# Windowed attention with a gated convolution layer on one core: where the probabilities are normalised and transposed, and in which form the value product writes x

## The chip, the cores and the metric

The kernel runs on one core of a Trainium2 chip. PE is TensorE (matmuls and transposes, results in the eight banks of PSUM), DVE is VectorE, ACT is ScalarE, SP only issues loads. The metric is device time in microseconds (us): the median of several executions. A profile is one more execution, taken by the hardware profiler; its span goes from the first to the last instruction.

## The reference, cut to what matters

Eight batches of eight heads with 64 channels; 512 local and 32 global positions. A local query attends to the 32 global keys and to local keys at most 32 positions away; a global query attends to everything. The 576 rows of each batch then go through a gated layer with 512 channels.

```python
s_l = np.concatenate([s_lg, np.where(np.abs(i - j) <= 32, s_ll, -1e9)], axis=-1)
e = np.exp(s_l - s_l.max(-1, keepdims=True))
a_l = e / (e.sum(-1, keepdims=True) + 1e-9)
out_l = a_l @ np.concatenate([v_g, v_l], axis=2)     # out_g likewise, over all 544 keys
x = rows of (out_g, out_l), heads side by side       # 576 x 512 for each batch
gate = sigmoid(sum(conv_w[k] * xp[:, k:k + S, :] for k in range(5)))   # causal, xp padded in front
out = (gate * (x @ w_val)) @ w_out
```

## The kernel before, in words

**Units.** The work on local queries is cut into 32 units u: one batch and two heads (128 channels). The 512 queries of a unit are 16 chunks of 32; each chunk sees 128 keys, 32 global ones and 96 local ones. A half h of a unit is one head.

**Steps of a unit**, by the names of the order: `s` (l_s, L581): the scores, 32 fp32 matmuls on tiles of 64 rows and 32 columns. `mx` (l_max, L593): DVE adds the mask, negates and writes the rows to `pm` in SBUF, with the row minimum. `exp` (l_exp, L600): ACT, in place. `t` (l_t, L606): PE transposes `pm` into PSUM, four 128x128 for each half. `tc` (l_tc): a copy to `pts` in SBUF, on ACT (L416) or DVE (L418). `av` (l_av, L617): 32 matmuls with the probabilities as weights (128 x 32) and 65 columns of v; the 65th is a column of ones, so the row sums come out beside the products. `den`, `rec` (L626, L630): their reciprocals. `norm` (l_norm, DVE L640 or eight small ACT operations L638): products times reciprocals, to `xs` in SBUF. `xt` (l_xt, L646): four PE transposes. `xc` (l_xc): a copy of the transposed x to SBUF. `halo`: the four columns ahead of it.

**The gated layer.** `xh`, `xl` (L678) split x into two fp32r parts. `tap` and four `conv` steps (L682, scalar_tensor_tensor over 128x512) make the convolution on DVE; for units 0 and 1 (NPC = 2) PE makes it by five matmuls with diagonal matrices (`pc`, L707; diagonals by ACT, L696). `sig` is the sigmoid. For each group of four units (a batch), `g1` (L731) multiplies x by w_val in 16 parts of three matmuls (xh·wvh, xl·wvh, xh·wvl); `gv`, `gh`, `gl` (L739, L745) multiply by the gate and split; `g2` (L771) multiplies by w_out in the same way; `ob` copies the result out of PSUM, and `st` stores it. The 32 global queries of each batch have their own steps (`gs`, `gmax`, `gexp`, `gt`, `gtc`, `gav`, `gden`, `grec`, `gnorm`, `gx`, `gxc`), and their rows go through the gated layer at the very end (g1.g, g2.g).

**What sets the order.** A string ORDER (L61 to L159) lists all steps, with PSUM banks behind @ and, where there is a choice, the engine behind a colon. A class Plan goes through it with costs, and from them puts zero-fills of PE into early gaps; the order of each engine is that of the string. Loads go over SP in the order of the string; pools give buffers in rings (`pm` three, `pts` two, `xs` one).

```python
on_pe(T.matmul(ax[32 * j:32 * j + 32, h, E1 * i:E1 * i + E1], pts[:, h, i, 32 * j:32 * j + 32],
         vt[:, block_win(4 * i + j), h, :], start=True, stop=True))
```

Of the kernel before, what the change touches and what calls it, by code (L numbers as in the profile page):

```python
# [76 lines left out]
t7.0@4 w7.s0:ACT w7.s1 g2.0.0.0@0 gtc1.1 tc7.0 gh.0.2 norm6 w6.s6 t7.1@2 w7.s2 w6.s7 tc7.1 gav1.1 xh4 gl.0.2 w7.s3 iq10
w6.high iv9 gden1 xc5 av7@6 den7 xt6@4 xh5 iq11 w7.s4 rec7 g2.0.0.1 grec1 w7.s5 gnorm1 gh.0.3 w7.s6 norm7:ACT gl.0.3
g2.0.0.2 s8@12 s9@53 gx1@6 xt7@7 w7.s7 w7.high mx9.0 tap4:ACT g2.0.0.3 gxc1 g2.0.1.0@5 mx9.1 g2.0.1.1 exp9.1 g2.0.1.2
t9.1@3 halo4 mx8.0 iv8 mx8.1 g2.0.1.3 xl4 ob.0.0 exp8.1 tc9.1 tap5:ACT conv4.0 halo5:ACT g2.0.2.0@6 ob.0.1:DVE conv4.1  # L80
gs2@20 gmax2.0 t8.1@5 conv4.2 st.0.0 exp8.0 st.0.1 g2.0.2.1 exp9.0 iv11 g2.0.2.2 t8.0@2 g2.0.2.3 g2.0.3.0@3 tc8.0 tc8.1
t9.0@5 gexp2.0 g2.0.3.1 xl5 ob.0.2 conv5.0 gmax2.1 tc9.0 av8@0 conv5.1 conv4.3 conv5.2 xc6 tap6 iv10 halo6:ACT conv5.3
av9@4 gexp2.1 s10@62 den8 rec8 den9 norm8 xh6:DVE gt2.0@0 xc7 xt8@7 gtc2.0 g2.0.3.2 xh7 iq12 mx10.0 mx10.1 halo7 xl6
exp10.0 g2.0.3.3 exp10.1 iq13 conv6.0 s11@26 tap7:ACT rec9 norm9 mx11.0 exp11.0 gav2.0@0 gt2.1@4 g1.1.0.0@1 mx11.1
t10.1@2 conv6.1 gtc2.1 t10.0@6 xl7 iq14 g1.1.0.1 g1.1.0.2 tc10.0 iq15 tc10.1 gav2.1 conv6.2 exp11.1 conv7.0 av10@4 iv12
t11.0@2 conv6.3 xc8:DVE conv7.1 gden2 xt9@7 tc11.0 conv7.2 conv7.3 g1.1.0.3 den10 g1.1.1.0@2 sig4 sig5 g1.1.1.1 g1.1.1.2
grec2 gnorm2 g1.1.1.3 ob.0.3:DVE gv.1.0 xc9 gh.1.0 g1.1.2.0@3 rec10 xh8:DVE tap8:ACT iv13 g1.1.2.1 sig6 g1.1.2.2
tap9:ACT t11.1@7 sig7 gx2@6 g1.1.2.3 norm10 xl8 gl.1.0 gv.1.1 gs3@40 gv.1.2 s12@32 gh.1.1:DVE st.0.3 gxc2 gmax3.0 tc11.1
av11@4 iv14 xt10@7 iq16 mx12.0 g1.1.3.0@3 mx12.1 halo8 exp12.0 den11 gl.1.1 exp12.1 g1.1.3.1 g1.1.3.2 gmax3.1 conv8.0
st.0.2 t12.0@2 gexp3.0 conv8.1 rec11 t12.1@6 g1.1.3.3 tc12.1 conv8.2 gv.1.3 s13@01 gh.1.2:DVE tc12.0 mx13.0 gl.1.2  # L90
conv8.3 mx13.1 norm11:ACT av12@2 gt3.0@4 exp13.0 g2.1.0.0@6 iv15 xt11@0 gh.1.3 halo9:ACT gl.1.3 xh9 xl9 den12 g2.1.0.1
xc10 g2.1.0.2 conv9.0 gtc3.0 rec12 g2.1.0.3 g2.1.1.0@7 s14@14 t13.0@5 norm12 tap10 exp13.1 conv9.1 g2.1.1.1 gexp3.1 xh10
mx14.0 conv9.2 g2.1.1.2 exp14.0 tc13.0 conv9.3 xl10 iq17 t13.1@1 g2.1.1.3 xt12@5 g2.1.2.0@2 ob.1.1:DVE mx14.1 halo10
# [984 lines left out]
```

## Time and profile before

| | us |
|---|---|
| three executions, median | 360.92 |
| lowest, highest | 359.85, 362.54 |
| span of the profiled execution | 358.4 |

The page's times are those of the profiled execution, whose span is 2.5 us below the median of the executions; a change is worked out against the span and then set beside the median. Busy time of an engine is the time in which any of its instructions runs; the start-to-start distance of neighbours is shorter than an instruction's length, since its end lies under the next one.

### The profile page before, as it was taken

To read this page: it belongs to the slowest core of one execution; us is meant where nothing else is said; L and a number is where in the kernel's file an instruction comes from. 1 tells how busy PE (TensorE), PEld (TensorE's weight loads), DVE (VectorE), ACT (ScalarE), POOL (GpSimd) and SP (SyncE) were. 2 spreads that over 40 slices of the span, in tenths; PEclk is the share of its full clock that TensorE was granted. 3 is DMA by queue.
4 is the path that set the end of the run, shared out by engine and by line. 5 is a ranking of instruction groups with operands and counts; after the bars stand their busy time and mean duration, and the time that the engine had idled before them with its cause. 6 is when DMAs were issued, how large, how long until landed. Compare 5 with 4: busy or idle time off the path is not lost.

```text
span 358.4 us, 14856 instructions
## 1 busy us (share of the span) xinstructions
PE 351.0 (98%) x6355; PEld 280.3 (78%) x6355; DVE 315.0 (88%) x1079; ACT 252.3 (70%) x630; POOL 0.8 (0%) x7
## 2 busy tenths in 40 slices
PE   8989999999999999999999999999999999999995
PEld 4647678778878788887878887888878888888895
DVE  4899999889989997998999989997897997995972
ACT  2999998996997888956766767976585585542030
POOL 0000000000000000000000000000000000000000
PEclk9999999999999999999999999999999999999999
DMA  8985677778897458822377157930790110020122
GB/s 277 400 327 171 230 267 262 251 231 299 268 302 251 141 183 289 335 92 85 131 266 260 59 202 251 347 131 28 241 381 8 62 58 2 31 89 32 59 77 71
DMA packets 21906, 66.75 MB, mean 186 GB/s; under 512 B 2384, under 2 KB 4944, under 8 KB 21840
## 3 DMA queue, kind: packets, MB, share of 16 engines
q1 hardware_dynamic: 16800, 56.86, 45.8%
q10 hardware_dynamic: 5040, 8.94, 6.8%
q8 instruction: 50, 0.82, 0.9%
q14 instruction: 16, 0.13, 0.1%
HBM read 56.87 MB, written 8.91 MB: 184 GB/s over the span
## 4 chain that ended last, share of the span: by engine, by line
PE 93%; DMA 4%; DVE 2%; ACT 1%; issue 0%; DVEq 0%
PE psum L731 27%; PE psum L771 25%; PE psum L581 8%; PE psum L617 8%; PE psum L606 8%; PE psum L646 4%; PE psum L545 3%; DMA v<-in_vw_dram 3%; PE psum L507 2%; PE psum L707 2%; PE psum L525 2%; PE psum L527 1%; DMA craw<-in_convT_dram 1%; PE psum L756 1%; DVE pm L593 1%; ACT pm L600 0%
## 5 line engine op out<-in xcount | busy, mean ns | idle before, releaser
L600 ACT ACTIVATE pm<-pm,mx 128x128 f32<-128x128 f32 x256 | 80.7, 399 | 16.2 <-DVE mx L593 16.0
L682 DVE SCALAR_TENSOR_TENSOR gate<-xc,cw,gate 128x512 f32<-128x512 f32 x120 | 88.2, 746 | 1.7 <-ACT gate L409 0.9
L593 DVE CUSTOM_DVE_ANT_0 pm<-psum,mask 128x128 f32<-128x128 f32 x256 | 57.6, 285 | 4.5 <-PE psum L581 4.3
L771 PE MATMUL psum<-woh,gh 128*128 128x512 f32 x128 | 53.7, 419 | 0.0
L731 PE MATMUL psum<-xh,wvh 128*128 128x512 f32 x128 | 52.9, 414 | 0.0
L731 PE MATMUL psum<-xl,wvh 128*128 128x512 f32 x128 | 50.7, 396 | 0.0
L731 PE MATMUL psum<-xh,wvl 128*128 128x512 f32 x128 | 50.5, 394 | 0.0
L771 PE MATMUL psum<-woh,gl 128*128 128x512 f32 x128 | 50.2, 392 | 0.0
L771 PE MATMUL psum<-wol,gh 128*128 128x512 f32 x128 | 50.1, 391 | 0.0
L416 ACT COPY pts<-psum 128x512 f32<-128x512 f32 x51 | 29.2, 590 | 15.3 <-PE psum L606 15.1
L606 PE MATMUL psum<-ident,pm 128*128 128x128 f32 x256 | 38.7, 277 | 0.7 <-ACT pm L600 0.7
L606 PEld LDWEIGHTS psum<-ident,pm 128*128 128x128 f32 x256 | 29.8, 140 | 10.7 <-ACT pm L600 2.9
L581 PE MATMUL psum<-qk 64*32 64x128 f32 x2048 | 36.9, 277 | 0.8 <-DMA qk<-in_qk_dram 0.5
L581 PEld LDWEIGHTS psum<-qk 64*32 64x32 f32 x2048 | 28.9, 107 | 9.1 <-issue 4.3
L617 PEld LDWEIGHTS psum<-v,pts 128*32 128x32 f32 x2048 | 30.5, 109 | 6.9 <-issue 3.3
L617 PE MATMUL psum<-v,pts 128*32 128x65 f32 x2048 | 34.5, 221 | 1.2 <-issue 0.8
L739 DVE TENSOR_TENSOR gv<-psum,gate 128x512 f32<-128x512 f32 x32 | 22.0, 687 | 9.3 <-PE psum L731 8.9
L731 PEld LDWEIGHTS psum<-xh,wvl 128*128 128x128 f32 x128 | 24.0, 188 | 5.4
L771 PEld LDWEIGHTS psum<-woh,gl 128*128 128x128 f32 x128 | 24.0, 188 | 5.3
L731 PEld LDWEIGHTS psum<-xh,wvh 128*128 128x128 f32 x128 | 24.1, 189 | 4.6
L731 PEld LDWEIGHTS psum<-xl,wvh 128*128 128x128 f32 x128 | 24.2, 189 | 4.2
L771 PEld LDWEIGHTS psum<-woh,gh 128*128 128x128 f32 x128 | 24.2, 189 | 4.1 <-DVE mx L593 0.2
(118 smaller groups left out, 559.0 us busy)
## 6 DMA issues: line engine op xcount, KB each, us to landing
qk<-in_qk_dram SPq DMA_DIRECT2D x31, 624.0 KB, 4.7
v<-in_vw_dram SPq DMA_DIRECT2D x30, 520.0 KB, 5.7
v<-in_vw_dram SPq DMA_DIRECT2D x30, 455.0 KB, 6.4
out_dram<-ob ACTq DMA_DIRECT2D x32, 256.0 KB, 2.2
wraw<-in_w_val_dram SPq DMA_DIRECT2D x4, 512.0 KB, 12.3
wraw<-in_w_out_dram SPq DMA_DIRECT2D x4, 512.0 KB, 4.6
v<-in_vw_dram SPq DMA_DIRECT2D x2, 975.0 KB, 12.2
qk<-in_qk_dram SPq DMA_DIRECT2D x1, 320.0 KB, 3.2
```

Of the source, the lines that this page charges most:

```text
L416: A.copy(out, in_)
L545: on_pe(T.matmul(ag[SG * c:SG * c + SG, :], pgt[:k, s, SG * c:SG * c + SG], vt[:k, w, h, :], start=(n == 0), stop=(n == len(steps) - 1)))
L581: on_pe(T.matmul((sx, sy)[h][32 * j:32 * j + 32, i, :], qkt[rows, q_col(m):q_col(m) + 32], qkt[rows, k0:k0 + P], start=True, stop=True))
L593: V.tensor_tensor_reduce(out=pm[:, h, i, :], in0=s[:, i, :], in1=mask[:, i, :], op0=ALU.add, op1=ALU.min, scale=-SCALE, scalar=3.0e38, acc ...
L600: A.activation(out=pm[:, h, i, :], in_=pm[:, h, i, :], func=AF.Exp, bias=mx[:, c:c + 1], scale=-1.0)
L606: on_pe(T.transpose(pt[:, i, :], pm[:, h, i, :], ident))
L617: on_pe(T.matmul(ax[32 * j:32 * j + 32, h, E1 * i:E1 * i + E1], pts[:, h, i, 32 * j:32 * j + 32], vt[:, block_win(4 * i + j), h, :], start ...
L646: on_pe(T.transpose(xt[:, P * i:P * i + P], xs[:, i].rearrange("p h d -> p (h d)"), ident))
L682: V.scalar_tensor_tensor(out=acc, in0=xc[:, k:k + SL], scalar=cw[:, u % NDT, k:k + 1], in1=acc, op0=ALU.mult, op1=ALU.add)
L731: on_pe(T.matmul(box["pv", e], w[:, e, t * P:t * P + P], x, start=(t == 0 and q == 0), stop=(t == NDT - 1 and q == 2)))
L739: V.tensor_tensor(out=box["gv", e], in0=box["pv", e], in1=gates[x0 + e], op=ALU.mult)
L771: on_pe(T.matmul(box["po", r], g[:, e, rs], w[:, e, :], start=(e == 0 and q == 0), stop=(e == NDT - 1 and q == 2)))
```

## The change

What it does:
- Row sums come from the exponential itself (`accum_out`), no longer from a column of ones. `den` and `rec` work on them.
- `norm` multiplies the probabilities `pm` in place (a half is 128x512; DVE one operation, or ACT four), ahead of the transpose; 26 halves on DVE and 38 on ACT.
- `t` is now l_turn: DVE transposes the 32x32 blocks of a half (128x512) from `pm` to `pts`. PE's transposes of the probabilities and the `tc` copies are gone.
- `av` takes v as weights (32 keys by 64 channels) and the probabilities as columns, in 52 matmuls with 128, 96, 64 or 32 columns, and writes x transposed, 128 columns in each of four banks. `xt` and `xs` are gone; `xc` reads those four banks, always on ACT.
- The host lays out queries, keys and values anew: qk 768 KB for a unit in one load (before 624; the first unit's in three pieces of 320, 160 and 144), v 455 KB in one load (before 975, in two). Global scores run over 640 columns in place of 544.
- The convolution of units 0 to 3 is on PE (NPC 2 to 4), with ten more diagonals on ACT.
- The ORDER string is a new one, and the Plan is gone: it is run as it stands. DVE has 2 output copies (before 14), 12 gh casts (17), 8 xh casts (9), 7 taps (10), 9 halo copies (14); ACT has the others. 14 loads of ACT's function tables are left of 18, and 12 zero-fills of PE for 15 (beside two short ones, as before).

```diff
-NPC = 2
+NPC = 4
 def load_qk(u):
-        for a, b in zip((EARLY[0], 0, EARLY[1]), (EARLY[1], EARLY[0], QK)) if u == 0 else ((0, QK),):
-            transfer(t[:, a:b], qk[u, :, a:b])
+        transfer(t, qk[u])
...
 def l_exp(u, h):
-            A.activation(out=pm[:, h, i, :], in_=pm[:, h, i, :], func=AF.Exp, bias=mx[:, c:c + 1], scale=-1.0)
+            A.activation(out=pm[:, h, i, :], in_=pm[:, h, i, :], func=AF.Exp, bias=mx[:, c:c + 1], scale=-1.0,
+                         accum_out=mx[:, 8 + c:9 + c])
-    def l_t(u, h):
...
-            on_pe(T.transpose(pt[:, i, :], pm[:, h, i, :], ident))
-    def l_tc(u, h):
-        copy(f"tc{u}.{h}", st[u]["pts"][:, h], st[u]["pt", h])
+    def l_norm(u, h):
+        p, rec = st[u]["pm"][:, h], st[u]["mx"][:, 8 + R * h:8 + R * h + R]
+        if BY[f"norm{u}.{h}"] == "ACT":
+            for i in range(R):
+                A.activation(out=p[:, i, :], in_=p[:, i, :], func=AF.Copy, scale=rec[:, i:i + 1])
+        else:
+            V.tensor_tensor(out=p, in0=p, in1=rec.unsqueeze(2).to_broadcast([P, R, P]), op=ALU.mult)
+    def l_turn(u, h):
...
+        V.transpose(out=st[u]["pts"][:, h].rearrange("p i a q -> p (i a q)"),
+                    in_=st[u]["pm"][:, h].rearrange("p i c -> p (i c)"))
     def l_av(u):
-            for i in range(4):
-                for j in range(4):
-                    on_pe(T.matmul(ax[32 * j:32 * j + 32, h, E1 * i:E1 * i + E1], pts[:, h, i, 32 * j:32 * j + 32],
-                             vt[:, block_win(4 * i + j), h, :], start=True, stop=True))
+        x = st[u]["x"] = banks(f"av{u}", R)[:, :, :P]
+        def product(j, h, slot, first, count, at, step, last):
+            rows = slice(C * j, C * j + C)
...
+            on_pe(T.matmul(x[D * h:D * h + D, j, C * first:C * (first + count)], vt[rows, slot, h, :D], p,
+                           start=(slot == NS - 1), stop=last))
+        for slot in (NS - 1, 2, 3, 1, 4, 0, 5):
+            for n in range(8):
+                j, h = n % R, (n + n // R) % 2
...
-    def l_xt(u):
...
-            on_pe(T.transpose(xt[:, P * i:P * i + P], xs[:, i].rearrange("p h d -> p (h d)"), ident))
     def l_xc(u):
-        copy(f"xc{u}", xc[:, KW - 1:], bank(f"xt{u}"))
+        copy(f"xc{u}", xc[:, KW - 1:].rearrange("p (j q) -> p j q", j=R), st[u]["x"])
```

What stands on DVE before, in the middle of the program, about units 15 to 19 (L682 are convolution steps, L640 the normalisation, L418 a copy or cast, L678 the low part of x, L626 den):

```order
L411 TENSOR_SCALAR gate16_3309<-xc16_3272,cw_68 128x512
L682 SCALAR_TENSOR_TENSOR gate15_3297<-xc15_3063,cw_68,gate15_3297 128x512
L418 CAST xh16_3324<-xc16_3272 128x512
L682 SCALAR_TENSOR_TENSOR gate15_3297<-xc15_3063,cw_68,gate15_3297 128x512
L640 TENSOR_TENSOR xs17_3329<-psum_64,mx17_2846 128x512
L678 TENSOR_TENSOR xl16_3325<-xc16_3272,xh16_3324 128x512
L418 COPY pts19_3262<-psum_64 128x512
L682 SCALAR_TENSOR_TENSOR gate15_3297<-xc15_3063,cw_68,gate15_3297 128x512
L682 SCALAR_TENSOR_TENSOR gate16_3309<-xc16_3272,cw_68,gate16_3309 128x512 x2
L626 TENSOR_SCALAR mx18_3107<-psum_64 128x8
```

And what stands on DVE at the like place of the change (L510 convolution steps, L441 rec, L449 the normalisation of a half, L454 the block transpose):

```order
L510 SCALAR_TENSOR_TENSOR gate15_3210<-xc15_3167,cw_68,gate15_3210 128x512
L510 SCALAR_TENSOR_TENSOR gate14_3260<-xc14_3087,cw_68,gate14_3260 128x512
L441 RECIPROCAL mx16_2684<-mx16_2684 128x8
L510 SCALAR_TENSOR_TENSOR gate14_3260<-xc14_3087,cw_68,gate14_3260 128x512
L449 TENSOR_TENSOR pm17_2938<-pm17_2938,mx17_2939 128x512
L510 SCALAR_TENSOR_TENSOR gate14_3260<-xc14_3087,cw_68,gate14_3260 128x512
L510 SCALAR_TENSOR_TENSOR gate15_3210<-xc15_3167,cw_68,gate15_3210 128x512
L449 TENSOR_TENSOR pm16_2683<-pm16_2683,mx16_2684 128x512
L454 STREAM_TRANSPOSE pts16_3328<-pm16_2683 128x512 x2
```

The copy of transposed probabilities out of PSUM has left DVE, the normalisation reads and writes SBUF, and two block transposes follow it for each unit.

What stands on PE before, about unit 21's scores (L581), with the transposes of x (L646) and of probabilities (L606) among the first products of a batch (L731):

```order
L581 MATMUL psum_64<-qk21_3039 32x128 x32
L646 MATMUL psum_64<-ident_66,xs19_3551 128x128 x4
L731 MATMUL psum_64<-xh15_3070,wvh_74 128x512
L731 MATMUL psum_64<-xl15_3071,wvh_74 128x512
L731 MATMUL psum_64<-xh15_3070,wvl_75 128x512
L606 MATMUL psum_64<-ident_66,pm20_3494 128x128 x4
L731 MATMUL psum_64<-xh12_2740,wvh_74 128x512
```

And on PE about unit 21's scores in the change (L414 the scores, L465 the value product in its new form, L586 the second product):

```order
L586 MATMUL psum_64<-woh_77,gl3_3426 128x512
L414 MATMUL psum_64<-qk21_3265 32x128 x32
L465 MATMUL psum_64<-pts18_3608,v18_2886 64x128 x8
L465 MATMUL psum_64<-pts18_3608,v18_2886 64x96 x16
L465 MATMUL psum_64<-pts18_3608,v18_2886 64x64 x16
L465 MATMUL psum_64<-pts18_3608,v18_2886 64x32 x12
L586 MATMUL psum_64<-woh_77,gh3_3425 128x512
```

No transposes are left on PE among the local units' steps; 52 matmuls make a unit's value product.

## Rows read from the trace of the kernel before

**Rows 1.** The page: busy us of each engine (share of the span), instructions.
```profile
PE 351.0 (98%) x6355; PEld 280.3 (78%) x6355; DVE 315.0 (88%) x1079; ACT 252.3 (70%) x630; POOL 0.8 (0%) x7
```
**Rows 2.** The page: the chain of waits that ended last, by engine.
```profile
PE 93%; DMA 4%; DVE 2%; ACT 1%; issue 0%; DVEq 0%
```
**Rows 3.** Stretches: length, busy us of PE, PEld, DVE, ACT, POOL; clock, DMA share, GB/s.
```profile
0.00:20.00 20.00, 17.52 (x331) 11.08 (x331) 14.09 (x74) 12.59 (x36) 0.85 (x7) 1.00 0.94 343
...
320.00:340.00 20.00, 20.00 (x89) 16.37 (x88) 15.36 (x34) 4.61 (x8) 0.00 (x0) 1.00 0.15 54
340.00:358.40 18.40, 14.68 (x98) 13.27 (x96) 9.55 (x25) 3.39 (x8) 0.00 (x0) 0.99 0.23 72
```
**Rows 4.** Timeline of PE at 151 us: start, length, operation.
```profile
150.98 0.40 PE L731 MATMUL psum<-xh,wvl 128*128 128x512 f32 x1
151.21 0.60 PE L606 MATMUL psum<-ident,pm 128*128 128x128 f32 x4
151.57 0.48 PE L731 MATMUL psum<-xh,wvh 128*128 128x512 f32 x1
151.89 0.40 PE L731 MATMUL psum<-xl,wvh 128*128 128x512 f32 x1
```
**Rows 5.** Timeline of PE from 14 to 28 us.
```profile
14.55 1.11 PE L617 MATMUL psum<-v,pts 128*32 128x65 f32 x64 [0.44 <-DMA v<-in_vw_dram]
15.59 1.16 PE L581 MATMUL psum<-qk 64*32 64x128 f32 x64
16.49 1.18 PE L507 MATMUL psum<-qk 64*32 64x384 f32 x32
...
24.08 3.60 PE L707 MATMUL psum<-xc,diag 128*128 128x512 f32 x8
27.52 0.49 PE L525 MATMUL psum<-ident,pg 128*96 128x128 f32 x3
```
**Rows 6.** Timeline of DVE at 103 us.
```profile
102.70 0.37 DVE L418 CAST xh<-xc 128x512 fp32r<-128x512 f32 x1
102.99 0.68 DVE L640 TENSOR_TENSOR xs<-psum,mx 128x512 f32<-128x512 f32 x1
103.59 0.68 DVE L678 TENSOR_TENSOR xl<-xc,xh 128x512 fp32r<-128x512 f32 x1
104.19 0.68 DVE L745 TENSOR_TENSOR gl<-gv,gh 128x512 fp32r<-128x512 f32 x1
```
**Rows 7.** Groups of DVE: busy us, mean ns of one; idle before.
```profile
L682 DVE SCALAR_TENSOR_TENSOR gate<-xc,cw,gate 128x512 f32<-128x512 f32 x120 | 88.2, 746 | 1.7 <-ACT gate L409 0.9
L514 DVE CUSTOM_DVE_ANT_0 pg<-psum,zero 128x544 f32<-128x544 f32 x16 | 11.5, 720 | 1.9 <-PE psum L507 1.7
L418 DVE COPY pts<-psum 128x512 f32<-128x512 f32 x13 | 8.7, 686 | 2.0 <-PE psum L606 1.8
```
**Rows 8.** DMA issues: count, KB each, median us to landing.
```profile
qk<-in_qk_dram SPq DMA_DIRECT2D x31, 624.0 KB, 4.7
qk<-in_qk_dram SPq DMA_DIRECT2D x1, 320.0 KB, 3.2
```
**Rows 9.** Timeline of DVE: the last convolution steps of a unit.
```profile
320.00 3.10 DVE L682 SCALAR_TENSOR_TENSOR gate<-xc,cw,gate 128x512 f32<-128x512 f32 x4
```
**Rows 10.** Timeline of PE: the first product of the global rows begins.
```profile
342.95 0.28 PE L731 MATMUL psum<-xgh,wvh 128*128 128x256 f32 x1
```
**Rows 11.** Groups of ACT: busy us, mean ns of one; idle before.
```profile
L600 ACT ACTIVATE pm<-pm,mx 128x128 f32<-128x128 f32 x256 | 80.7, 399 | 16.2 <-DVE mx L593 16.0
L416 ACT COPY pts<-psum 128x512 f32<-128x512 f32 x51 | 29.2, 590 | 15.3 <-PE psum L606 15.1
L638 ACT ACTIVATE xs<-psum,mx 128x64 f32<-128x64 f32 x72 | 15.7, 334 | 3.7 <-DVE mx L630 3.2 <-PE psum L646 0.4
L600 ACT ACT_TABLE_LOAD x8 | 10.3, 1283 | 1.7 <-DVE mx L593 1.6
L416 ACT COPY xc<-xgT 128x4 f32<-128x4 f32 x16 | 3.1, 202 | 0.0
```

More of the change, by code (lines that the diff above doesn't have):

```diff
@@ L77 @@
[L77 to L81, printed above, removed]
@@ L157 @@
-gh.g.1:DVE gh.g.2 gl.g.1 g1.g.3.1 g1.g.3.2 g1.g.3.3 st.7.0 gl.g.2 gv.g.3 g2.g.0.0@0 gh.g.3:DVE g2.g.0.1 g2.g.0.2 gl.g.3
-g2.g.0.3 ob.g.0:DVE st.g.0 g2.g.1.0@1 g2.g.1.1 g2.g.1.2 g2.g.1.3 ob.g.1 st.g.1
+E1 = D + 1
+GQ = NC
+K0 = GQ + 1
+PAIRED = (3, 6, 9, 12, 15)
+KEYS = [x for c in range(NC) for x in ((c, -1) if c % 3 == 2 else (c,))] + [x for c in PAIRED for x in (c, -1)]
+NB = K0 + len(KEYS)
+AT = {c: K0 + c + c // 3 for c in range(NC)}
+WITH_G = {c: K0 + NC + NC // 3 + 2 * n for n, c in enumerate(PAIRED)}
@@ L188, in kind @@
-def kind(name):
-    k = name.rstrip("0123456789.")
-    return "tc1" if k == "tc" and name.endswith(".1") else k
-class Task:
-    __slots__ = ("name", "eng", "cost", "deps", "take", "give", "emit", "end", "start", "lock", "spare", "alts")
-    def __init__(self, name, eng, cost, deps, take, give, emit, lock):
-        self.name, self.eng, self.cost, self.deps = name, eng, cost, deps
-        self.take, self.give, self.emit, self.lock = take, give, emit, lock
-        self.start = self.end = None
@@ L495, in g_s @@
         units = [loads[u][0] for u in range(NDT * b, NDT * b + NDT)]
-        s = [pair(f"gs{b}.{h}").rearrange("p a c -> p (a c)")[:, P:P + 544] for h in range(2)]
+        s = [banks(f"gs{b}", 2, h).rearrange("p a c -> p (a c)")[:, C:C + GC] for h in range(2)]
         for part in range(2):
@@ L854, in attention_moe @@
-    plan.add("first", "DMA", int(arrival) - LAG["DMA"], lambda: None)
-    for k in range(2 * NDT):
-        weight(k)
-        if k >= NDT:
-            plan.add(f"wi{k}", "SP", 450, wraws[k], [f"s{k - NDT + WO}"], take=[("pm", f"w{k}")])
-        elif ("w", k) not in first:
-            plan.add(f"wi{k}", "SP", 450, wraws[k], [f"wi{k - 1}"] if k % 2 and ("w", k - 1) not in first else [])
-        if ("w", k) not in first:
-            plan.add(f"wl{k}", "DMA", 1350, lambda: None, [f"wi{k}"])
@@ L943, in attention_moe @@
-    plan.add("cw", "DVE", 1410, taps, ["craw"], take=[("mx", "cv")], give=[("mx", "cv")])
-    plan.given("start", 0.0)
-    last = "start"
-    for b in range(B):
-        units = range(4 * b, 4 * b + 4)
-        for u in units:
-            plan.add(f"sig{u}", "ACT", 530, lambda u=u: sigmoid(gates[u]),
-                     [f"fix{v}" if v < NHF else f"conv{v}.{KW - 2}" for v in units] + ([f"sig{u - 1}"] if u % 4 else []))
-        last = moe(b, SL, 4 * b, lambda t, b=b: [f"xl{4 * b + t}"], lambda e, b=b: [f"sig{4 * b + e}"], last,
-                   lambda r, o, b=b: A.dma_start(out[b, SG + r * P:SG + r * P + P, :], o))
@@ new lines, in _layout @@
+    vl = v_l.reshape(NU, 2, NC, C, D)
+    vg = v_g.reshape(NU, 2, SG, D)
+    vw = np.zeros((NU, R, C, NS, 2, E1), v_l.dtype)
+    vw[..., D] = 1.0
+    for j in range(R):
+        for slot in range(NS):
+            c = R * j - 1 + slot
+            if slot == NS - 1:
+                vw[:, j, :, slot, :, :D] = vg.transpose(0, 2, 1, 3)
+            elif 0 <= c < NC:
+                vw[:, j, :, slot, :, :D] = vl[:, :, c].transpose(0, 2, 1, 3)
+    vw = vw.reshape(NU, P, NS, 2, E1)
+    mask = np.zeros((P, R, R, C), np.float32)
@@ L1050, in _layout @@
+    r = np.arange(C)
+    for m in range(NC):
+        j, i = divmod(m, R)
+        for a in range(R - 1):
+            c = m - 1 + a
+            far = np.abs((C * m + r)[:, None] - (C * c + r)[None, :]) > 32
+            mask[C * j:C * j + C, i, a][far if 0 <= c < NC else np.full((C, C), True)] = NEG
     convT = moe_conv_w.T.reshape(NDT, P, KW).transpose(1, 0, 2).reshape(P, NDT * KW)
```

826 lines of the change are left out of this document (275 added, 551 removed).

## The prediction

> **What bounds the kernel now.** I read the busy times first: PE works 351.0 of 358.4 us, DVE 315.0, ACT 252.3 [rows 1]. The reader is to see that PE has only 358.4 - 351.0 = 7.4 us left, so whatever leaves PE is gained until another engine stops it, and DVE, with 43.4 us idle, is the first that can. The chain of waits says the same: 93% of it is PE [rows 2]. The table of stretches then shows where DVE's idle time lies [rows 3]: 20.00 - 14.09 = 5.9 us at the start, 4.64 + 8.85 = 13.5 us in the last 38.4 us, and so 43.4 - 5.9 - 13.5 = 24.0 us between 20 and 320. The two ends will stay (loads, and products that wait for nothing of DVE's); the 24 us are DVE waiting for a PE that is full. All windows were granted the full clock but for 0.99 in the last one, so no clock term enters.
>
> **What leaves PE.** Four transposes in the middle of products begin at 151.21, the next product at 151.57, and the one after it 0.32 later, where products stand 0.23 apart [rows 4]: 0.36 + 0.09 = 0.45 us for a group. The change drops three groups in each of 32 units (two of the probabilities, one of x): 96 x 0.45 = 43.2 us.
>
> **What comes to PE.** Convolution of units 2 and 3: ten fp32 matmuls in the program, 20 in the trace (each fp32 matmul stands there twice), at (27.52 - 24.08) / 8 = 0.43 us [rows 5]: 8.6. The global scores take 640 columns in place of 544: 8 x 1.10 x 96/544 = 1.6 (1.18 with its end under the next one's start [rows 5]). Three zero-fills fewer: about -0.8.
> The value product changes its form. Before, a unit is 32 matmuls on four tiles, 8 x 65 = 520 columns on each, twice: 1040 columns in 15.59 - 14.55 = 1.04 us; the scores are 64 pieces on eight tiles, 1024 columns in 16.49 - 15.59 = 0.90 [rows 5]. Both are near 1 ns for a column of a tile, though one has 16.3 ns for a piece and the other 14.1. The new product has 52 matmuls (104 pieces) on eight tiles, up to 512 columns on each, so 1024 again. By columns it costs 0.90 to 1.04: nothing more. By pieces it would cost 104 x 16.3 = 1.69, +0.65 a unit. I take columns, since the scores already have eight tiles and pieces of less than 16.3 ns, and keep +0.65 x 32 = 20.8 us as the upper end. PE's sum: 351.0 - 43.2 + 8.6 + 1.6 - 0.8 = **317.2**.
>
> **What leaves DVE.** An operation's last 0.08 us lie under the next one's start, so I count from start to start: 0.60 for 128x512 with two operands, in PSUM or not, and 0.29 to 0.34 for a cast inside SBUF [rows 6]; a copy from PSUM lasts as long as the former (686 ns [rows 7]). The order of the change takes from DVE 13 copies of transposed probabilities, 12 output copies and 9 x copies, 34 x 0.60 = 20.4; 8 convolution steps at 0.74 [rows 7], 5.9; 6 casts, 2.0; 3 taps, 1.2; five halo copies and smaller operands, about 1.1. Together -30.6.
>
> **What comes to DVE.** 64 block transposes of 128x512. No row has one. Lower bound: the cast's 0.34, if it runs as fast as the fastest fp32 operation inside SBUF. Upper: 1.20, twice the 0.60, if the block has to be filled and then emptied. I take 0.60, as nearly all DVE rows of this width have it: 38.4. Three more normalisations (26 against 23), at 0.60 though both operands now lie in SBUF: 1.8. Sixteen global maxima over 640 columns, 11.5 us for 544 [rows 7]: +0.1 each, 1.6. Together +41.8, net +11.2: DVE's sum is **326.2**, 9 above PE's. DVE becomes the bound.
>
> **The sum.** The span is DVE's start, its work up to the last convolution step, and the tail behind that.
> Start: 5.9 us idle as now, plus about 1: the first unit's qk comes in one piece of 768 KB, not in pieces of which the first has 320. From 320 to 624 KB the landing goes from 3.2 to 4.7 us [rows 8], 4.9 ns a KB, so it is up to 2.2 later; some of that lies under the convolution weights and the mask. Bounds 0 and 2.2.
> Work: in the trace the last step ends at 320.00 + 3.10 = 323.1 [rows 9]; from there DVE has 15.36 + 9.55 - 3.1 = 21.8 us left, which stays as it is. 326.2 - 21.8 = 304.4.
> Tail: by the new order 10 parts of the last unit row's first product and 16 of the second follow, three matmuls of 0.23 each, 26 x 0.70 = 18.2; then the global part, 342.95 [rows 10] to 358.4, 15.45: 33.65.
> 5.9 + 1 + 304.4 + 33.65 = **345** against the profiled 358.4. The median is 360.9, 2.5 more than the span; with that, **347**.
> This costs DVE's waits in the middle at nothing. Their cover is PE's slack: PE needs 317 of 345 and is now ahead of DVE, where before DVE waited for it. If the 24 us stayed, the time would be 371.
>
> **ACT** has 252.3. It loses 51 copies (29.2) and 72 small normalisations (15.7), gains 152 normalisations of 128x128 at 0.31 (the exponentials' 399 ns less 0.09) = 47.1, 27 copies and casts at 0.59 = 15.9, ten diagonals at 0.40 and small copies = 5.7, and loses four table loads of 1.28, 5.1 [rows 11]: 271. Its 256 exponentials now also write their row sums. A reading of the accumulator is an instruction that no ACT row has; I take 0.10 (half of the smallest ACT operation, 202 ns [rows 11], the rest being covered by its neighbours), with 0 and 0.20 as bounds: 271, **297** or 322. With 297 ACT has 14 us less work than it has time for up to the tail. So it is hidden, but only just, and an exponential that comes late makes norm, transposes and the value product late.
>
> **Moved with it.** Exp to norm now runs over ACT and DVE alone, without the visits to PE, so the probabilities' buffer (three of them) is held until the transposes have read it. The value product takes four PSUM banks in one piece where the old one took two, while the banks of the transposes are free. Loads shrink by 12 MB in all, at no price, as PE and not the queue set the middle.
>
> **Rivals.**
> *Row sums make ACT the bound*: at 0.20 each ACT has 322; with its own start (7.4 us idle in the first 20 [rows 3]) and the tail less what it does in it, about 355, so 358. For it: ACT's margin is thin. Against it: short operations hide part of their length here. 0.11.
> *The transposes take half the rate* (slower): at 1.20 DVE has 364.6, the span is 383, the time **385**. It is slower than before by 1% from (364.5 - 347)/64 + 0.60 = 0.87 us on. For it: no row shows a transpose. Against it: the only longer 128x512 rows on DVE are the convolution's 0.74. 0.06.
> *The transposes run like a cast*: DVE 309.6, then PE and ACT hold it at about **335**. 0.06.
> *The value product is limited by pieces*: PE 338, +7.4 idle and a little of DVE's waits: **351**. 0.07, inside the range.
> *Each new piece costs twice an old one* (slower): its weights are 64 columns, not 32, and if loading them sets the pace, 104 x 32.6 ns = 3.4 us a unit in place of 1.04, +75 on PE: 392 + 7.4 + 2.5 = **402**. It decides from (364.5 - 2.5 - 7.4 - 317.2) / 32 + 1.04 = 2.2 us a unit on, 21 ns a piece. Against it: in [rows 5] pieces follow each other at 14.1 and 16.3 ns, and columns explain both. For it: pieces of 32 rows and 64 columns of weights are in no row. 0.05.
> By the Trainium skill, "TensorE: Matmul & The Clock Gate", section "Wait — 56ns, not 53.3ns?", start-to-start never drops below about 25 ns however small a matmul is. By that figure the product would take 2.6 us a unit, an estimate, and the time would come near 377. The trace disagrees for pieces that lie on different tiles (14.1 ns), and the row decides.
> *DVE keeps waiting in the middle* though PE has room, on single handoffs: 371. 0.02.
> That the change doesn't do what it says is no rival: in its order the transposes stand on DVE and those of PE are gone.
>
> **How the numbers follow.** Forecast (342 to 352) 0.60; row sums 0.11; pieces 0.07; transposes at half rate 0.06; transposes like a cast 0.06; doubled pieces 0.05; waits 0.02; the rest, about as before, 0.03. The range 338 to 361 takes in the forecast, the row sums and the pieces, and the start's and the exponentials' bounds; it leaves out both other rates of the transposes, the doubled pieces and the waits, 0.19. A difference of 1% is about what a measurement of this kernel can tell from none: 357.3 and 364.5. Faster: 0.60 + 0.07 + 0.06 + 0.03 of the row sums = 0.76. Same: 0.08 + 0.03 = 0.11. Slower: 0.06 + 0.05 + 0.02 = 0.13.
>
> **What would show it.** PE busy near 317 and DVE near 326, with DVE over 95% busy between 20 and 310 and PE no longer; transposes 0.68 us long, 0.60 apart; a value product of 104 pieces in about 1 us; ACT below 300, its readings of the accumulator about 0.1 apart from the exponentials. The forecast is wrong if the transposes stand over 0.7 apart, if the value product takes over 1.7, if ACT is busy for over 310, or if idle time on DVE waits for ACT's sums. A hole in PE's first 20 us that lowers the granted clock would be a cost that I have not counted.

## The result and the profile after

| | before | after |
|---|---|---|
| median of the executions, us | 360.53 | 355.93 |
| profiled span, us | 358.4 | 354.5 |
| PE busy, us | 351.0 | 338.5 |
| DVE busy, us | 315.0 | 323.6 |
| ACT busy, us | 252.3 | 293.8 |

The kernel before was executed once more beside the changed one: 360.53 is the median of four. The ratio to it is 0.986, with a 95% interval from 0.982 to 0.990. The change makes the kernel faster by 1.4%, where 3.8% were forecast (347); the time lies inside the range, the size is a third of what was said.

The page of the changed kernel, busy time and chain of waits (before: [rows 1, 2]):

```profile
PE 338.5 (95%) x7268; PEld 262.8 (74%) x7268; DVE 323.6 (91%) x1088; ACT 293.8 (83%) x942; POOL 1.0 (0%) x8
...
PE 81%; ACT 8%; DMA 6%; DVE 2%; issue 1%; ACTq 0%
```

DVE and ACT stand where they were put (326 and 297). PE stands 21 us above its 317, and it is still the chain.

The span cut at the first product of batch 0 (first column), of batch 2 and of batch 7; first the kernel before, then the changed one (columns as in [rows 3]):

```profile
0.00:44.40 44.40, 40.70 (x923) 27.00 (x923) 37.92 (x166) 36.66 (x103) 0.85 (x7) 1.00 0.79 282
44.40:138.80 94.40, 94.37 (x2038) 75.48 (x2034) 87.52 (x323) 82.03 (x209) 0.00 (x0) 1.00 0.74 244
138.80:321.00 182.20, 182.20 (x3223) 148.98 (x3223) 165.65 (x536) 125.86 (x306) 0.00 (x0) 1.00 0.44 158
321.00:358.40 37.40, 33.68 (x181) 28.84 (x179) 23.95 (x56) 7.79 (x16) 0.00 (x0) 1.00 0.19 64
```

```profile
0.00:46.30 46.30, 37.62 (x960) 24.89 (x960) 36.80 (x158) 38.24 (x137) 0.96 (x8) 0.93 0.77 273
46.30:134.70 88.40, 86.31 (x1899) 64.09 (x1900) 84.78 (x313) 83.47 (x275) 0.00 (x0) 1.00 0.47 158
134.70:317.30 182.60, 181.08 (x4232) 145.00 (x4232) 175.32 (x560) 162.73 (x512) 0.00 (x0) 1.00 0.42 138
317.30:354.50 37.20, 33.47 (x181) 28.81 (x180) 26.74 (x60) 9.31 (x20) 0.00 (x0) 0.98 0.22 77
```

The reader is to see the idle time of PE: 8.7 us in the first stretch in place of 3.7, and 2.1 and 1.5 in the next two, which were full before. The lengths of the stretches can't be set against each other one by one. The cuts follow the gated layer, and the attention is spread over them in another way: before, the value products of 5, 11 and 16 units stand in the first three (64 pieces each), in the changed kernel those of 4, 8 and 20 (104 pieces each), as the counts on their lines in the third stretch show (busy us of PE and PEld):

```profile
138.80:321.00 182.20, 16.71 (x1024) 15.11 (x1024) 1.00 0.44 158
134.70:317.30 182.60, 30.36 (x2080) 28.18 (x2080) 1.00 0.42 138
```

So 182.2 and 182.6 are alike because the changed kernel does less for a unit there, but for four units more. What the change gains shows only in sums over the whole program. The variants of the changed kernel below all have its 4, 8 and 20, and can be compared with it stretch by stretch.

What keeps PE full: the value product of a unit in the middle of the program, in the changed kernel (from its start to the next operation's, 106.44 - 104.99 = 1.45 us; before, 0.93 to 1.05 where nothing interrupts it, as the 1.04 in [rows 5], and 1.00 on average):

```profile
104.99 1.52 PE L465 MATMUL psum<-pts,v 32*64 32x128 f32 x104
106.44 0.38 PE L378 MATMUL psum<-v,pgt 128*32 128x65 f32 x12
```

### The profile page after: what moved, and what is told of

It is laid out like the page before. It is cut to its first block, busy times and chain, and to the rows that moved or that the text cites. A ratio compares the mean times of both kernels' runs of the same rounds, so it can differ in the third digit from the quotient of the medians.

```text
span 354.5 us, 16954 instructions
## 1 busy us (share of the span) xinstructions
PE 338.5 (95%) x7268; PEld 262.8 (74%) x7268; DVE 323.6 (91%) x1088; ACT 293.8 (83%) x942; POOL 1.0 (0%) x8
## 4 chain that ended last, share of the span: by engine, by line
PE 81%; ACT 8%; DMA 6%; DVE 2%; issue 1%; ACTq 0%
PE psum L586 26%; PE psum L549 24%; PE psum L465 13%; PE psum L414 8%; ACT pm L432 4%; PE psum L378 3%; PE psum L362 3%; DMA v<-in_vw_dram 3%; PE psum L343 2%; DMA wraw<-in_w_out_dram 2%; ACT pm L447 2%; DMA qk<-in_qk_dram 1%; PE psum L575 1%; PE psum L632 1%; PE psum L395 1%
## 5 line engine op out<-in xcount | busy, mean ns | idle before, releaser
L432 ACT ACTIVATE pm<-pm,mx 128x128 f32<-128x128 f32 x256 | 99.4, 392 | 1.3 <-DVE mx L425 0.6
L510 DVE SCALAR_TENSOR_TENSOR gate<-xc,cw,gate 128x512 f32<-128x512 f32 x112 | 81.6, 744 | 1.4 <-ACT xc L256 0.3
L465 PEld LDWEIGHTS psum<-pts,v 32*64 32x64 f32 x3328 | 45.8, 133 | 11.0 <-issue 7.1
L586 PE MATMUL psum<-woh,gh 128*128 128x512 f32 x128 | 52.7, 412 | 0.0
L465 PE MATMUL psum<-pts,v 32*64 32x64 f32 (+3 forms) x3328 | 49.4, 246 | 1.2 <-DMA v<-in_vw_dram 1.2
L586 PE MATMUL psum<-woh,gl 128*128 128x512 f32 x128 | 50.0, 391 | 0.0
L586 PE MATMUL psum<-wol,gh 128*128 128x512 f32 x128 | 49.9, 390 | 0.0
L432 ACT ACTIVATION_READ_ACCUMULATOR pm<-pm,mx 128x1 f32 x256 | 48.6, 190 | 0.0
L447 ACT ACTIVATE pm<-pm,mx 128x128 f32<-128x128 f32 x152 | 48.1, 391 | 0.1
L454 DVE STREAM_TRANSPOSE pts<-pm 128x512 f32<-128x512 f32 x64 | 43.9, 699 | 0.7 <-ACT pm L447 0.4
L414 PE MATMUL psum<-qk 64*32 64x128 f32 x2048 | 38.2, 281 | 3.8 <-issue 1.5
L414 PEld LDWEIGHTS psum<-qk 64*32 64x32 f32 x2048 | 30.3, 108 | 13.6 <-issue 5.5
L256 ACT COPY xc<-psum 128x512 f32<-128x512 f32 x32 | 18.6, 581 | 13.3 <-PE psum L465 6.9
L586 PEld LDWEIGHTS psum<-woh,gh 128*128 128x128 f32 x128 | 24.3, 190 | 5.9 <-issue 1.1
L586 PEld LDWEIGHTS psum<-woh,gl 128*128 128x128 f32 x128 | 24.0, 188 | 5.4
L256 ACT COPY ob<-psum 128x512 f32<-128x512 f32 x30 | 17.2, 578 | 12.6 <-PE psum L586 10.4
```

The source lines that it names most:

```text
L256: A.copy(out, in_)
L414: on_pe(T.matmul(s[h][C * j:C * j + C, i, :], qkt[rows, C * m:C * m + C], blocks(qkt[rows], b, (C * far, 2), (C * near, 2), (1, C)), start ...
L432: A.activation(out=pm[:, h, i, :], in_=pm[:, h, i, :], func=AF.Exp, bias=mx[:, c:c + 1], scale=-1.0, accum_out=mx[:, 8 + c:9 + c])
L447: A.activation(out=p[:, i, :], in_=p[:, i, :], func=AF.Copy, scale=rec[:, i:i + 1])
L454: V.transpose(out=st[u]["pts"][:, h].rearrange("p i a q -> p (i a q)"), in_=st[u]["pm"][:, h].rearrange("p i c -> p (i c)"))
L465: on_pe(T.matmul(x[D * h:D * h + D, j, C * first:C * (first + count)], vt[rows, slot, h, :D], p, start=(slot == NS - 1), stop=last))
```

## The experiments

Theory P, after the result: TensorE still holds the time, since a value product costs 0.47 us more than before, by the number of its pieces and not by their columns. Rivals: VectorE at 96% (D), ScalarE's row sums (A), and the lower clock early on (K). Four kernels take work from one engine at a time. Ratios are to the kernel before, timed again beside each group of runs (medians 359.5 to 360.4).

**av_narrow.** All pieces but those of the global keys get 32 columns.

```diff
-product(j, h, slot, i0, i1 - i0 + 1, slot + ...)
+product(j, h, slot, i0, 1, slot + ...)
```

> The changed kernel with the value product's pieces cut in width, not in number: all matmuls but those of the global keys take 32 columns (one query chunk) in place of 32 to 96, so part of the value product is left out. 104 pieces in the trace as before, columns for a tile 2 x 304 in place of 2 x 496. Theory P (TensorE is the bound again, because each piece of the value product takes about 14 ns whatever its width): the product stays at 1.45 us a unit and the time stays within 1% of 355.9. Rival C (columns set its length, as the prediction had it, at 1.45 / 992 = 1.46 ns each): 0.9 us a unit, 17 us less on TensorE, time near 345.

352.52 us, 0.980 of before (0.977 to 0.983); span 350.9. The product takes 106.07 - 104.72 = 1.35 us:

```profile
104.72 1.42 PE L465 MATMUL psum<-pts,v 32*64 32x128 f32 x104
106.07 0.43 PE L378 MATMUL psum<-v,pgt 128*32 128x65 f32 x16
```

Columns fell by 39%, the length by 7%. Neither expectation is exact: the columns beyond 32 are worth 0.10 of the 1.45 us, and the rest does not go with them.

**av_few.** 24 of the 52 matmuls of a value product stay.

```diff
-for slot in (NS - 1, 2, 3, 1, 4, 0, 5):
+for slot in (NS - 1, 2, 3):
...
-product(..., slot == (5 if j < R - 1 else 0))
+product(..., slot == 3)
```

> The changed kernel with only 24 of the 52 matmuls of a value product (global keys and two of the six slots), the rest left out: 48 pieces in the trace, columns for a tile 2 x 320. Takes work from TensorE alone. Theory P: 48 x 14 ns = 0.67 us a unit, 0.78 x 32 = 25 us less on TensorE; if TensorE is the bound in the steady part, the time falls until VectorE holds it, to about 344 (323.6 of VectorE, 7.8 idle at its start, 10.4 in the tail, 1.4 around the span). Rival D (VectorE at 96% or ScalarE's row sums set the pace): within 1% of 355.9, 352.4 to 359.5.

344.02 us, 0.956 of before (0.953 to 0.959); span 341.4. The product takes 107.55 - 106.68 = 0.87 us:

```profile
106.68 0.94 PE L465 MATMUL psum<-pts,v 32*64 32x128 f32 x48
107.55 0.33 PE L395 MATMUL psum<-ident,xg 128*128 128x128 f32 x1
```

That is not the 0.67 that was expected. From 48 to 104 pieces it is 0.58 us, 10.4 ns for each further piece, and 0.37 us do not go with their number; of these, 0.15 to 0.17 lie between the start of the last piece and the next operation. The 40 pieces that the new form has more than the old one are worth some 0.42 of its 0.47 us at that price.

The profile from the first product of batch 0 to that of batch 7, one stretch:

```profile
44.10:304.10 260.00, 253.69 (x4562) 190.01 (x4562) 257.67 (x871) 244.26 (x786) 0.00 (x0) 1.00 0.44 149
```

18.2 us less on PE (page: 320.3 busy) give 13.1 us of span. Then DVE holds the kernel: 257.67 of 260.00 us, 99%. Theory P's 344 came out, though the work that left PE was less than its 25 us: DVE sets that time, so PE's share did not matter to it.

**dve_less and act_less.** The convolution steps over 328 columns; and the exponentials without row sums.

```diff
-V.scalar_tensor_tensor(out=acc, in0=xc[:, k:k + SL], ..., in1=acc, ...)
+V.scalar_tensor_tensor(out=acc[:, :328], in0=xc[:, k:k + 328], ..., in1=acc[:, :328], ...)
```

```diff
 A.activation(out=pm[:, h, i, :], in_=pm[:, h, i, :], func=AF.Exp, bias=mx[:, c:c + 1], scale=-1.0,
-             accum_out=mx[:, 8 + c:9 + c])
+             )
-V.tensor_scalar(out=den, in0=den, scalar1=1e-9, scalar2=None, op0=ALU.add)
+V.tensor_scalar(out=den, in0=st[u]["mx"][:, 0:8], scalar1=1e-9, scalar2=None, op0=ALU.add)
```

> The changed kernel with each of VectorE's 112 convolution steps over 328 columns in place of 512 (the rest of the convolution left out): about 22 us less on VectorE, nothing else changed. Theory P (TensorE bound): 1 to 4 us off 355.9, not below 351. Rival D (VectorE bound, as the prediction had it): at least half of the 22 us comes off, 345 or less.

> The changed kernel without row sums from the exponentials: no reading of the accumulator, and the reciprocals are taken of the row minima, so the normalisation is not the reference's. 256 x 0.094 = 24 us less on ScalarE. Theory P (TensorE bound in the steady part, ScalarE in the first 46 us, where it is busy 38.2 of the 39.2 us from its first diagonal on): 2 to 5 us off 355.9, from the first 46 us. Rival A (ScalarE's row sums set the pace throughout): 12 us or more off, 344 or less.

353.66 us for the first (0.984, 0.980 to 0.988) and 356.05 for the second (0.990, 0.987 to 0.993); spans 351.6 and 353.9. The stretch of five batches in each, dve_less and then act_less:

```profile
132.40:314.50 182.10, 181.21 (x4233) 145.01 (x4232) 162.88 (x562) 163.26 (x513) 0.00 (x0) 1.00 0.42 139
```

```profile
134.20:316.80 182.60, 181.11 (x4233) 145.02 (x4233) 175.07 (x560) 150.42 (x373) 0.00 (x0) 1.00 0.41 138
```

12.4 us less on DVE, or 12.3 less on ACT, in the same 182 us: neither engine holds these batches. Of what dve_less gains (2.9 of 354.5) it has 2.6 by the first product, at 43.7 in place of 46.3. D and A fall for the steady part. act_less missed its expectation as well: its first product stands at 44.6, 1.6 us earlier and not 2 to 5, and 0.6 us of span are left of that at the end. So ACT's row sums hold 1.6 us of the start, and the end keeps little of it.

**npc2.** One part undone: the convolution of units 2 and 3 back on DVE.

```diff
-NPC = 4
+NPC = 2
-dg2 ... dg3 ... pc2.0@3 ... pc2.1 pc2.2 pc2.3 ... pc2.4 ... conv2.3:ACT
+tap2:ACT ... conv2.0 conv2.1 conv2.2 ... conv2.3   (unit 3 likewise)
```

> The changed kernel with one part undone: the convolution of units 2 and 3 back on VectorE (taps on ScalarE, no diagonals for them). TensorE loses 20 x 0.44 = 8.8 us of work between 47 and 60 us, VectorE gains 8 x 0.67 = 5.3, ScalarE loses about 2.6. Theory P (TensorE holds the time from 46 us on): 3 to 6 us off the time, near 351. Rival D (VectorE holds that stretch): 3 to 5 us slower, near 360. If neither: the two cancel, within 2 us of 355.9.

360.41 us, 1.0025 (0.9996 to 1.0054); span 357.9. It is the rival's case. The stretch from the first product of batch 0 to its second one:

```profile
45.60:84.80 39.20, 27.26 (x571) 19.86 (x571) 36.62 (x135) 30.58 (x98) 0.00 (x0) 0.78 0.32 112
```

The same stretch of the changed kernel:

```profile
46.30:79.50 33.20, 31.16 (x592) 20.47 (x592) 31.05 (x126) 31.43 (x103) 0.00 (x0) 1.00 0.40 135
```

Without the convolution on PE it takes 6 us more. DVE has 5.6 us more and works 93% of it; PE works 27.3 of 39.2 us and is granted 0.78 of its clock on average, a mean of its two levels, in place of 1.00. This early stretch is not PE's: here the convolution on PE, which the prediction costed at +8.6 on PE, is worth 3.4 us of span, by DVE's load and by the clock. The two shares were not taken apart.

**z_hole, av_first, av_first_z.** In its start the changed kernel's PE waits 5.6 us, and for a part of what follows it is granted the lower level (1.2 GHz), 0.83 on average from 20 to 40 us:

```profile
16.56 1.09 PE L414 MATMUL psum<-qk 64*32 64x128 f32 x58
23.27 1.30 PE L362 MATMUL psum<-ident,pg 128*128 128x128 f32 x5 [5.62 <-ACT pm L432]
24.50 2.30 PE L465 MATMUL psum<-pts,v 32*64 32x128 f32 x104
26.72 1.31 PE L378 MATMUL psum<-v,pgt 128*32 128x65 f32 x40
```

```profile
20.00:40.00 20.00, 16.73 (x480) 11.91 (x481) 19.21 (x70) 18.52 (x59) 0.00 (x0) 0.83 0.57 189
```

The first value product takes 26.72 - 24.50 = 2.22 us and not 1.45. Three edits of the order:

```diff
-... gt0.0@4 av0@0 ...
+... z6.2@2 z6.3@2 z6.4@2 gt0.0@4 av0@0 ...     (z_hole)
+... av0@0 gt0.0@4 ...                          (av_first)
+... z6.2@2 z6.3@2 av0@0 gt0.0@4 ...            (av_first_z)
```

> The changed kernel with 18 zero matmuls more on TensorE, in three groups of six ahead of the first transposes of global probabilities (bank 2, which nothing else holds then): they fill its hole from 17.6 to 23.3 us. Theory K (the lower clock after the hole costs time): the granted clock stays at 1.00 from 20 to 40 us, the first value product takes 1.5 us and not 2.3, and 2 to 3 us come off the time. Theory S (the first 46 us are held by ScalarE, busy 38.2 us there, so the clock costs little): the clock stays up, but the time changes by less than 1 us.

> The changed kernel with two neighbours on TensorE exchanged: the first value product ahead of the first transposes of global probabilities, for which TensorE waits until 23.3 us. The product can then start when the row minima of unit 3's first head are done (its bank 3), about 21.5 us in place of 24.5. If the start is worth what TensorE loses there (theory P), 1.5 to 3 us come off; if ScalarE holds the first 46 us (theory S), under 1 us.

> Both: the exchange and twelve zero matmuls in what is left of the hole. Theory P with K: the clock at 1.00 and 3 to 5 us off, near 351.5. Theory S: under 1 us off.

359.88 (0.999), 356.83 (0.990) and 358.58 us (0.997); spans 358.2, 356.3 and 356.5. None of them gained. z_hole and av_first_z are 4.0 and 2.7 us slower than the changed kernel, which neither theory had; av_first, 0.9 slower, is within what theory S allows. Yet z_hole did what it was made for; its stretches from 20 to 40 us and from batch 2 to batch 7:

```profile
20.00:40.00 20.00, 18.56 (x495) 12.35 (x494) 19.45 (x69) 20.00 (x66) 0.00 (x0) 1.00 0.67 218
...
134.30:321.00 186.70, 182.34 (x4232) 145.54 (x4232) 175.37 (x560) 163.22 (x512) 0.00 (x0) 1.00 0.40 135
```

The clock stays at 1.00 (2.4 GHz), and batch 0's products start at 43.9 and not 46.3. But the five batches, a hundred us later, take 186.7 and not 182.6, with 4.4 us of PE idle. Two of these holes:

```profile
142.27 0.70 PE L378 MATMUL psum<-v,pgt 128*32 128x65 f32 x33
143.74 0.32 PE L378 MATMUL psum<-v,pgt 128*32 128x65 f32 x7 [0.77 <-issue]
...
168.44 0.83 PE L343 MATMUL psum<-qk 64*32 64x480 f32 x11
170.05 0.50 PE L343 MATMUL psum<-qk 64*32 64x160 f32 x13 [0.78 <-issue]
```

They lie inside a group of like matmuls that waits for no other engine ("issue"). Counted from PE's first matmul in the trace, the holes of z_hole that exceed 0.6 us and lie inside a group of small matmuls, from 60 us on, stand at numbers 1371, 2010, 3160, 3799, 5075 and 5842: 639, 1150, 639, 1276 and 767 apart, each a multiple of 128 less 1 to 4 (some records are missing). av_first, which adds no matmul, has 182.6 for the five batches, av_first_z with 12 more has 186.7.

The trace shows what comes at the end of such a hole. Beside the loads and stores it holds transfers of 16384 bytes of the kind "instruction"; on queue q8 (the page's queue table: transfers, MB, share) there are

```profile
q8 instruction: 57, 0.93, 1.1%
```

in z_hole, 57 in the changed kernel, 50 before and 66 in before_split (a run further down). The matmuls in these traces are 7286, 7268, 6355 and 8403, so one transfer comes for every 127 to 128 of them, on average 6 us apart. Each of the six holes ends 1.25 to 1.50 us after the end of one of these transfers. That makes the holes waits for instructions; why these transfers come late was not followed.

**z_same and av_first_same.** The same with PE's count of matmuls kept.

```diff
-... z6.0@1 ... z6.1@2 ... gt0.0@4 av0@0 ...
+... y1.0@1 ... y1.1@2 ... y4.2@2 gt0.0@4 av0@0 ...
+if name[0] == "y": zeros(n, bank, fp32 zeros of 432 columns)   # two matmuls in the trace each
```

> z_hole again, but with as many matmuls on TensorE as the changed kernel has: its two groups of six zero matmuls (128x512) become two fp32 zero matmuls (128x432, two in the trace each), and four more stand in the hole, so 12 in the trace before and after, and every later matmul keeps its number. In z_hole the clock stayed up and the first product of batch 0 began at 43.9 us and not 46.3, but the five batches from 2 to 7 took 186.7 us in place of 182.6, with holes of 0.6 to 0.8 us inside groups of small matmuls that wait for nothing in the profile, at numbers that stand a multiple of 128 (give or take 4) apart. Theory N (TensorE's instructions come in blocks of 128 matmuls, and a block that ends inside a dense group is late): the five batches take 182 to 183 us again and the span is 352 to 354.5. Rival Z (having the clock up early changes the order of events later): still 186 and a span near 358.

> av_first_z (the first value product ahead of the first global transposes, zero matmuls in the hole) with the matmuls' numbers kept in the same way. Theory N: batches 2 to 7 in 182 to 183 us, span 352 to 353.5, time near 354, 1.5 to 2 us under the changed kernel. Rival Z: as av_first_z, 356.5.

354.39 us (0.984, 0.982 to 0.986) and 354.18 (0.988, 0.981 to 0.995); spans 352.4 and 352.4. z_same keeps the clock and the five batches:

```profile
20.00:40.00 20.00, 19.14 (x491) 11.96 (x491) 19.43 (x69) 20.00 (x65) 0.00 (x0) 1.00 0.65 227
132.70:315.20 182.50, 181.46 (x4232) 145.22 (x4231) 175.22 (x560) 162.78 (x512) 0.00 (x0) 1.00 0.41 138
```

The numbers of the matmuls decide, not the early clock: theory N holds. With them kept, filling the hole is worth 2.1 us of the profiled span and 1.5 between the medians. By their spans these two are the shortest kernels here that compute everything; their intervals and that of the changed kernel overlap.

**before_split.** What does a piece cost by itself? In the kernel before, each matmul of the value product cut in two.

```diff
-on_pe(T.matmul(ax[..., E1 * i:E1 * i + E1], pts[...], vt[:, block_win(4 * i + j), h, :], ...))
+for lo, hi in ((0, 33), (33, E1)):
+    on_pe(T.matmul(ax[..., E1 * i + lo:E1 * i + hi], pts[...], vt[:, block_win(4 * i + j), h, lo:hi], ...))
```

> The kernel before with each matmul of the value product cut in two (33 and 32 of its 65 columns): 128 pieces for a unit in the trace in place of 64, the same columns and results, nothing else changed. Theory P (13 to 14 ns for each piece once the pieces are short): 1.7 to 1.8 us a unit in place of 0.98, +0.75 x 32 = +24 us on a kernel that TensorE holds, time near 384. Rival C (columns set the length): within 2% of 360.

428.88 us, 1.190 (1.186 to 1.195). The expectation missed on both sides. Where nothing is late, 128 pieces take 16.10 - 14.69 = 1.41 us up to the scores, where 64 took 1.04 [rows 5], and not 1.7 to 1.8; from piece to piece it is 10.1 ns, where before it is 14.2. But in many units something is late:

```profile
14.69 1.48 PE L618 MATMUL psum<-v,pts 128*32 128x33 f32 x128
16.10 1.10 PE L581 MATMUL psum<-qk 64*32 64x128 f32 x58
...
166.43 2.18 PE L618 MATMUL psum<-v,pts 128*32 128x33 f32 x203
170.96 0.76 PE L618 MATMUL psum<-v,pts 128*32 128x32 f32 x53 [2.35 <-issue]
```

```profile
PE psum L618 <- issue: 23.0, 13, 3.4
...
PE psum L581 <- issue: 10.1, 7, 4.0
...
PE psum L545 <- issue: 2.9, 2, 1.8
```

(The waits: us in total, times, the longest.) The pieces themselves cost (1.41 - 1.04) x 32 = 12 us, 5.8 ns for each added one. 36.0 us on these three lines are holes of this kind ("issue"), up to 4.0 us each; in the kernel before the same view has 0.8. All 19 holes over 0.6 us inside a group of one line end 1.26 to 1.56 us after the end of an instruction transfer on q8, as in z_hole. How the other 20 of the 68 us divide between the lower clock (mean 0.96) and waits that follow from the holes was not settled.

**av_w32 and av_narrow_w32.** Why 13 ns in one form, 10 in the other? Half the weights in each matmul; av_narrow_w32 has av_narrow's edit as well.

```diff
-on_pe(T.matmul(x[D * h:D * h + D, ...], vt[rows, slot, h, :D], p, ...))
+on_pe(T.matmul(x[D * h:D * h + C, ...], vt[rows, slot, h, :C], p, ...))
```

> The changed kernel with 32 of the 64 columns of v as weights in each matmul of the value product (half of the channels left out); 104 pieces of the same widths. In before_split a piece with 128 rows and 32 columns of weights took 10.0 ns where nothing was late, in the changed kernel one with 32 rows and 64 columns takes 13.9. Theory W (the width of the weights sets a piece's price): 104 x 10 = 1.04 to 1.1 us a unit, and the span falls by about 10 us to 344. Rival I (a piece on eight tiles costs 13 to 14 ns whatever its weights): 1.45 us a unit and a span within 1.5 us of 354.5.

> Both: 32 columns of weights and 32 columns of probabilities in all but the global keys' matmuls (the rest left out), 104 pieces. Theory W: 1.0 us a unit or less, span 343 to 345. Rival I: 1.35 us as in av_narrow, span 351.

One execution each, 350.92 and 349.63 us; spans 349.0 and 347.8. The product, first of av_w32 and then of av_narrow_w32:

```profile
103.48 1.39 PE L465 MATMUL psum<-pts,v 32*32 32x128 f32 x104
104.80 0.32 PE L378 MATMUL psum<-v,pgt 128*32 128x65 f32 x8
```

```profile
103.12 1.25 PE L465 MATMUL psum<-pts,v 32*32 32x128 f32 x104
104.30 0.32 PE L378 MATMUL psum<-v,pgt 128*32 128x65 f32 x8
```

1.32 and 1.18 us. Neither theory holds alone: of 1.45 us, the weights' second half is worth 0.13 to 0.17 and the columns beyond 32 are worth 0.10 to 0.14. Of the 1.18 that are left, 1.05 lie from the first piece to the last, 10.2 ns a piece, the spacing of before_split; the rest is behind the last piece. So the two forms differed less than the expectation says: its 13.9 ns had the time behind the last piece in it, without which the changed kernel's pieces are 12.6 ns apart. The rows of the weights, 32 in the new form and 128 in the old one, were not varied.

## Why the prediction went wrong, step by step

- **What leaves PE**: right. From start to start, the transposes of before sum to 41.2 us over the span (43.2 predicted).
- **The value product**: the step that failed. "By columns it costs 0.90 to 1.04: nothing more." It costs 1.45 us against 1.00; over the span, from start to start, 47.2 us and not 32.1: +15.2. In the trace of before, the scores and the value product have 64 pieces and some 1030 columns each, so pieces and columns could not be told apart by these two rows, and I took the one that gave nothing. The third of [rows 5], which I used only for the global scores, has 32 pieces in 1.10 us (the next operation starts at 17.59), 34 ns a piece and 0.7 ns a column of a tile: it fits neither price alone, so the two had to be mixed. The other end, 1.69 us, was in the text with a chance of 0.07; that its PE sum of 338 meets the 338.5 is in part luck, since 15.2 of its 20.8 came from the value product and the rest from terms that were left out. Between ends that the rows cannot tell apart, half of 20.8 would have been the term.
- **Terms of PE that were left out**: the global value product (+1.8), the global transposes (+1.0) and the scores (+1.0) became longer. Convolution on PE: +9.0 (8.6 predicted). Global scores: +0.9 (1.6).
- **"Their cover is PE's slack"**, by which DVE's waits were costed at nothing, is the second step that failed. PE has 338.5 us of work and not 317; with the 7.4 that it had idle that is 346, as long as DVE's 345. So the value product and the terms left out bring PE level with DVE, and by their sums alone the span would still be 346 and not 354.5. The rest is waiting, which was costed at nothing: PE's idle time grows by 8.6 us to 16.0, 5.0 of them in the first stretch, and from 20 to 320 us DVE waits 12.7. That av_few, with PE at 320.3, comes to 341.4 and has DVE 99% busy, shows that the DVE sum itself (345) stands within some 1%, once PE has the slack that I gave it.
- **DVE's terms**: right. The transposes are 0.63 us apart and 699 ns long (0.60 and 0.68), DVE 323.6 (326.2):

```profile
L454 DVE STREAM_TRANSPOSE pts<-pm 128x512 f32<-128x512 f32 x64 | 43.9, 699 | 0.7 <-ACT pm L447 0.4
L432 ACT ACTIVATION_READ_ACCUMULATOR pm<-pm,mx 128x1 f32 x256 | 48.6, 190 | 0.0
```

- **ACT's row sums**: right. The reading is 190 ns long but costs 0.093 us from start to start (0.10 taken), ACT 293.8 (297). Without them the steady batches don't move, and the kernel as a whole gains 0.6 us of span (act_less).
- **The start**: DVE is idle for 7.75 us of the first 20 (6.9 predicted). The hole in PE and its clock, named as "a cost that I have not counted", are real: 2.1 us of the profiled span (z_same).
- **The tail**: 37.2 us from batch 7's first product, 37.4 before; the last convolution step ends at 322.95, and the 31.6 behind it are 2.1 less than predicted.
- **The doubled piece**: not so; from the first piece to the last, pieces on different tiles follow each other in 10.1 to 14.8 ns on average in these runs. The floor of 25 ns that the Trainium skill gives in "TensorE: Matmul & The Clock Gate", section "Wait — 56ns, not 53.3ns?", is contradicted by them for such pieces.

The balance on PE: 41.2 go; 15.2 + 9.0 + 0.9 + 3.8 come, with -0.2 in smaller ones, so work falls by 12.5. Idle time grows from 7.4 to 16.0: 5.0 in the first stretch, 2.1 and 1.5 in the two behind it. 12.5 - 8.6 = 3.9, the span's gain. Convolution on PE is in this sum as work, but npc2 shows that it pays: without it the span is 3.4 us longer.

## What to carry to other kernels

A tiled product has several prices: here its number of pieces, their columns and weights, and a part for the whole group. Where the rows at hand have pieces and columns in one proportion, a new shape's price lies between the two, and the sum should carry that. Before a bound is declared to have moved to another engine, ask what margin the old one is left with (here 28 us on paper, 15 of which one unpriced term took), and take work from one engine at a time to see which one the time follows. An edit that adds a few matmuls early can cost more much later than it gains where it stands: compare stretches of the same work, not only the end, and count first what work stands in a stretch.

## What the runs showed of the hardware

- PE's stream of matmuls has holes at fixed numbers, multiples of 128 apart, when such a number falls into a dense group of small pieces: 0.6 to 0.8 us each after 90 us in z_hole, up to 4.0 us in before_split, where 128 pieces pass in 1.3 us. Each of them ends 1.25 to 1.56 us after a 16384-byte instruction transfer, of which there is one for every 127 to 128 matmuls. Adding 12 or 18 matmuls at 20 us brought more of them and cost 4.1 us after 134 us; keeping the count took that back.
- The row sum of an exponential over 128 columns costs ScalarE 0.093 us from start to start, and VectorE's 32x32 block transpose of 128x512 takes 0.63, hardly more than the 0.60 of a two-operand pass of that width [rows 6].
- Small matmuls on different tiles: the added piece costs 5.8 ns where 64 are cut into 128 of half the columns, and 10.4 ns from 48 to 104 pieces; with 32 columns and 32 weights pieces stand 10.2 ns apart. The old value product takes 0.93 us where the global one follows it without a wait, and 1.02 to 1.05 before other operations.
